# One burst of attention a step, and the squares of q and k as a stage of their own, in a fused attention and gated feed-forward kernel

## The chip, the core and the metric

The kernel runs on one core of a Trainium2 chip. A core has five engines that work from queues of their own: TensorE (PE in the profile; its weight loads are PEld), VectorE (DVE), ScalarE (ACT), GpSimd (POOL) and SyncE (SP), which here issues the transfers. TensorE writes its results to PSUM, from which DVE and ACT read; everything else lies in SBUF, and the inputs, the output and scratch copies in DRAM. The metric is the device time of one execution in microseconds. All times below are of this kind, or are starts and durations from one profiled execution.

## The reference

Two computations follow each other. The first is attention with random features: for 8 batches, 8 heads, 576 positions and 64 numbers a head,

```
q_s, k_s = q * scale, k * scale                # scale = 64 ** -0.25
phi(x)   = exp(x @ omega.T - |x|^2 / 2 - max) / sqrt(128)
kv       = sum over positions of phi(k_s)^T v       # 128 x 64 a head
z        = sum over positions of phi(k_s)           # 128 a head
attn     = (phi(q_s) @ kv) / (phi(q_s) @ z + 1e-6)
```

The maximum is taken over the 128 features of each row. The second is a gated feed-forward network over the 4608 tokens (batch and position) of 512 numbers that attention gives, with 1536 inner columns:

```
g   = x @ w_gate
out = (silu(g) * (x @ w_val)) @ w_out
```

All of it is float32 outside; the kernel does the feed-forward matmuls as three products of a high and a low part each.

## The kernel before

**Steps.** The rows of q and k are cut into groups of 256 rows of a pair of heads (plus a group of rests), and a *step* handles two groups: two of k in the first six steps, then one of q and one of k, at the end two of q. There are 72 steps, and a few more to run out. One group passes through functions that are called in different steps: `load` three steps ahead; `st_transpose` (four transposes on TensorE into the PSUM tile pt, ACT copies it to x, POOL squares the loaded rows into sq); `st_project` (16 small matmuls into pp); `st_max` (DVE sums the squares, L419, takes the maxima of pp, L426, and forms the exponent's bias, L428 and L429); `st_exp` (eight exponentials on ACT, L440). A group of k then goes to `k_accumulate` two steps later (matmuls into kvacc, and where a half of the heads of a batch is complete, `kv_finalize`, in which ACT copies kvacc to kvr, L456). A group of q goes one of two ways. For batches 0 to 3, `q_transpose` (ptq, ACT copies it to qt), a step later `q_mult` (po, with the denominator as a 65th column; DVE forms dn, its reciprocal and the normed rows xn, L590 to L593), and again a step later `q_out` (transposes of xn into xt, from which ACT and DVE make the high and low parts, or ACT a copy xo for DRAM). For batches 4 to 7, `q_den` and `q_norm` do the division with POOL and DVE, from z laid out over all partitions: `kv_finalize` transposes z (zp, L462), ACT copies it, and it goes to DRAM (zd); `load_z` brings it back spread out (zt).

**Two halves.** The first 25 steps (`n < EARLY`) call the functions in the order of the tuple `CLOSE`. From then on the order is `GROUPED`, a *mixed* step: attention's functions, and at each place `SHARE` a share of the feed-forward work, which `give` takes from the generator `stream`, and of the conversion of the weights (`tick`, whose generator `convert_all` gives five DVE operations, L270 to L278, for each piece, between an ACT one, L268, and a POOL one, L280). In a mixed step before the change attention comes in two places: most of it at the head, and `q_norm` and `q_mult` between the third and the fourth SHARE.

**Buffers.** PSUM tiles rotate by tag. `ps_att` has one buffer (tag b: po, zp, and ptq of the first group), `ps_tr` one (tag t: pt, xt), kvacc one (tag kv), pp two (tag pp), the feed-forward tiles three (tag m). A tile is written again only when its readers are done. In SBUF, nat (the loaded rows) has three buffers, sq two, st six.

**Feed-forward.** Tokens come in nine tiles of 512. Five go through `stream`, in visits of 72 matmuls (g and v, L659) and 36 (o, L668, summed by DVE into acc, L697) each. The last four go in two pairs by `pair_rounds`, with seven products instead of eight (L874): DVE adds a kept part to a product (`plus`, L971), and one PSUM tile a takes several products in turn. While the second of the first pair's six visits runs, `next_x` loads the second pair's rows, and after each `one_down` it gives one of eight subtractions (L829) that prepare the seven factors; they are used in that pair's last visit.

**The order of the queues.** The code gives an order of calls. In each engine's queue the instructions stand in an order that the framework makes from that order and from what it takes to be ready; in the trace, an instruction of DVE, ACT or POOL that waits holds those behind it (at 874.75 us DVE has waited 5.30 us for a transfer, with a sum behind it whose product was done).

Of the kernel before, what the change touches and what calls it, by code (L numbers as in the profile page):

```python
# [11 lines left out]
F32 = mybir.dt.float32  # L12
# [4 lines left out]
ALU = mybir.AluOpType  # L17
# [6 lines left out]
def kernel(  # L24
# [73 lines left out]
    def ps_att(name, shape):  # L98
        return ps_a.tile(shape, F32, name=name, tag="b")
# [275 lines left out]
    sts = {}  # L375


    def st_transpose(n):
        if n >= NS:
            return  # L380
        nat = nats.pop(n)
        pt = ps_tr(f"pt_{n}", [P, 2, G])
        for i in range(2):
            for c in range(CH):
                nc.tensor.transpose(  # L385
                    pt[:, i, c * P : (c + 1) * P], nat[:, i, c].rearrange("p h d -> p (h d)"), ident
                )
        x = att.tile([P, 2, G], F32, name=f"x_{n}", tag="x")

        st = att.tile([P, 4, 2, CH, 2], F32, name=f"st_{n}", tag="st", bufs=6)  # L390
        sq = att.tile([P, 2, CH, 2, D], F32, name=f"sq_{n}", tag="sq")
        nc.gpsimd.tensor_tensor(sq, nat, nat, op=ALU.mult)  # L392
        nc.scalar.copy(x, pt)  # L393
        sts[n] = x, st, sq
        return True

    def st_project(n):
        if n >= NS:
            return
        x, st, sq = sts[n]  # L400

        new = ps_moe if n < EARLY and n % 2 else ps_proj
        pp = [new(f"pp{hh}_{n}", [P, 2, CH, M]) for hh in range(2)]
        for i in range(2):
            for c in range(CH):
                for hh in range(2):
                    r = slice(hh * D, (hh + 1) * D)
                    nc.tensor.matmul(  # L408
                        pp[hh][:, i, c, :], x[r, i, c * P : (c + 1) * P], omT[r], start=True, stop=True
                    )  # L410
        sts[n] = st, sq, pp
        return True

    def st_max(n):
        if n >= NS:
            return
        st, sq, pp = sts[n]

        nc.vector.tensor_reduce(  # L419
            st[:, 0].rearrange("p i c h -> p (i c h)"),  # L420
            sq.rearrange("p i c h d -> p (i c h) d"),
            axis=AX.X,
            op=ALU.add,
        )
        for hh in range(2):
            nc.vector.tensor_reduce(st[:, 1, :, :, hh], pp[hh], axis=AX.X, op=ALU.max, negate=True)  # L426
        s0, s1, s2, s3 = (st[:, j].rearrange("p i c h -> p (i c h)") for j in range(4))
        nc.vector.scalar_tensor_tensor(s2, s0, SQC, s1, op0=ALU.mult, op1=ALU.add)  # L428
        nc.vector.scalar_tensor_tensor(s3, s0, -SQC, s2, op0=ALU.mult, op1=ALU.add)  # L429
        return True  # L430

    def st_exp(n):
        if n >= NS:
            return
        st, _, pp = sts.pop(n)
        for i, (kind, b, g) in enumerate(steps[n]):
            ph = att.tile([P, CH, 2 * M], F32, name=f"ph{i}_{n}", tag=f"ph{i}", bufs=3)
            for hh in range(2):
                for c in range(CH):
                    nc.scalar.activation(  # L440
                        ph[:, c, hh * M : (hh + 1) * M], pp[hh][:, i, c, :],
                        AF.Exp, bias=st[:, 3, i, c, hh : hh + 1], scale=1.0,
                    )
            box[kind, b, g] = ph
        return True
# [7 lines left out]
    def kv_finalize(b, a2):  # L453
        acc = kvacc.pop((b, a2))
        raw = att.tile([P, 4, VW], F32, name=f"kvr{b}_{a2}", tag="kvr", bufs=4)
        nc.scalar.copy(raw, acc)  # L456
        for j in range(2):
            kvst[b, 2 * a2 + j] = raw[:, 2 * j : 2 * j + 2, :]
        if b >= BPOOL:

            zp = ps_att(f"zp{b}_{a2}", [4, P])
            nc.tensor.transpose(zp, raw[:, :, D], ident)  # L462
            zs = att.tile([4, P], F32, name=f"zs{b}_{a2}", tag="zs")
            nc.scalar.copy(zs, zp)
            zd = dram.tile([4, P], F32, name=f"zd{b}_{a2}", tag="zd", bufs=4)
            nc.sync.dma_start(zd, zs)
            zds[b, a2] = zd

    zds = {}
    zbc = {}  # L470

    def load_z(n):

        for _, b, g, gr in slots(n, "q"):
            if g == 0 and b >= BPOOL:
                zt = att.tile([P, 2, 4, M], F32, name=f"zt{b}", tag="zt")
                for a2 in range(2):
                    nc.sync.dma_start(
                        zt[:, a2], zds.pop((b, a2)).rearrange("(o h) m -> o h m", o=1).broadcast_to([P, 4, M])
                    )  # L480
                    zbc[b, a2] = zt[:, a2]
# [29 lines left out]
    def q_norm(n):  # L511
        n -= NLAG
        for _, b, g, gr in slots(n, "q"):
            if b < BPOOL:
                continue
            dn = dns.pop((b, g))
            phv = box["q", b, g].rearrange("p c (h m) -> p (c h) m", m=M)
            nc.gpsimd.tensor_tensor(
                phv, phv,
                dn[:, 2].rearrange("p c (h o) -> p (c h) o", o=1).broadcast_to([P, 2 * CH, M]),  # L520
                op=ALU.mult,
            )
# [266 lines left out]
    sevens = {}  # L789

    factors, ahead = {}, {}

    def first_x():

# [26 lines left out]
    def next_x(r):  # L821

        for half, names in ((0, ("b11", "t1")), (1, ("b21", "b22"))):
            for j, name in zip(PAIRS[r], names):
                nc.sync.dma_start(ahead[name], x_dram[j][:, half * CH : (half + 1) * CH, :])
        yield
        for o, a, b in (("t3", "b22", "t1"), ("t1", "t1", "b11"), ("t2", "b22", "t1"), ("t4", "b21", "t2")):
            for c in range(CH):
                nc.vector.tensor_tensor(ahead[o][:, c], ahead[a][:, c], ahead[b][:, c], op=ALU.subtract)  # L829
                yield  # L830

    def new_factors():
# [51 lines left out]
    def pair_rounds(todo):  # L884
# [51 lines left out]
        for vi, (r, k_, pf) in enumerate(pair_visits):  # L936
# [20 lines left out]
            for i, use in ((0, gate), (1, value)):  # L957
# [10 lines left out]

                def plus(n, ps, name):
                    o = sl[n] if i == 0 else kp[:, 3]  # L970
                    nc.vector.tensor_tensor(o, ps, keep[name], op=ALU.add)  # L971
                    use(n, o)

                a, c, d = (ps_w.tile([P, T], F32, name=f"{e}{vi}_{i}", tag="w") for e in "acd")
# [35 lines left out]
    def give(us):  # L1010
# [15 lines left out]
    SHARE = None  # L1026
    CLOSE = (
        st_project,
        q_norm,
        q_out,  # L1030
        lambda n: st_transpose(n + 1),
        q_mult,
        lambda n: k_accumulate(n, 0),
        st_max,
        q_transpose,
        lambda n: k_accumulate(n, 1),
        st_exp,
# [1 line left out]
    )  # L1039
    GROUPED = (  # L1040
        q_out,
        st_project,
        q_transpose,
        lambda n: k_accumulate(n, 0),
        lambda n: k_accumulate(n, 1),
        st_max,
        st_exp,
        q_den,
        lambda n: st_transpose(n + 1),
        SHARE,  # L1050
        SHARE,
        SHARE,
        lambda n: q_norm(n + 1),
        q_mult,
        SHARE,
        SHARE,
        SHARE,
# [6 lines left out]
    for n in range(LAV):  # L1064
        load_v(n)
    load(2)
    st_transpose(0)
    for n in range(NN):
        load(n + LA)
# [56 lines left out]
```

## Time and profile before

| what | value |
|---|---|
| median of 3 runs | 1218.34 us (1216.6 to 1220.92) |
| the profiled execution | 1219.54 us |
| its span, first to last instruction | 1217.8 us |
| mean granted TensorE clock | 0.987 |
| TensorE busy | 1173.9 us, 96% |
| weight loads | 969.5 us, 80% |
| ACT, DVE, POOL busy | 660.9 us (54%), 647.1 us (53%), 585.0 us (48%) |

Rows of the profile name an instruction by its engine, its line (L419), what it writes and reads (st<-sq), and how often it occurs. In a timeline the columns are start, duration, engine, line, operation, and in brackets the engine's idle time before it and what ended that. A table of waits has the waiting line, what it waited for, the total, the number of times and the longest. Matmuls overlap, so that a matmul of 0.39 us may start 0.23 us after the one before, and TensorE's busy share says little by itself; its idle times and the starts of its instructions say more. The granted clock is TensorE's, 1.00 being full speed.

### The profile page before, as it was taken

The page shows a single profiled execution, that of the slowest core. Times are in us where ns is not written, and L with a number is a line of the kernel's source. Part 1 is how long each engine was busy: PE and PEld are TensorE (multiplying, and loading weights), DVE is VectorE, ACT ScalarE, POOL GpSimd, SP SyncE. Part 2 cuts the span into 40 slices and gives each one's busy share as a digit, 9 for nine tenths or more (in the row PEclk, how much of TensorE's full clock was granted, in tenths as well). Part 3 has the DMA queues.
Part 4 walks back from the last instruction along what each step waited for, and adds up shares of the span by engine and source line. Part 5 has one row for each costly group of instructions (what it writes and reads, how often), then busy time and mean ns, then how long its engine had stood idle before and what let it go on. Part 6 is the DMA issues. An engine that isn't in the chain of part 4 may idle for free.

```text
span 1217.8 us, 18846 instructions
## 1 busy us (share of the span) xinstructions
PE 1173.9 (96%) x6705; PEld 969.5 (80%) x6705; DVE 647.1 (53%) x1231; ACT 660.9 (54%) x1461; POOL 585.0 (48%) x500
## 2 busy tenths in 40 slices
PE   6999999999999999999999999999899999999998
PEld 5888887888787678878888877878688888888886
DVE  5588886364656763434333354174545456545544
ACT  4687866574465555466555666353454445454431
POOL 3343442254344645545454585444565553555541
PEclk9799999999999999999999999999999999999999
DMA  6556656253544433244222211334321111312103
GB/s 151 125 132 157 168 146 186 50 153 86 170 113 119 119 86 93 71 112 101 66 62 81 67 60 45 88 103 138 96 55 58 48 49 26 104 52 53 52 18 69
DMA packets 174109, 113.52 MB, mean 93 GB/s; under 512 B 125856, under 2 KB 144320, under 8 KB 174016
## 3 DMA queue, kind: packets, MB, share of 16 engines
q1 hardware_dynamic: 174016, 112.32, 34.1%
q8 instruction: 53, 0.87, 0.3%
q14 instruction: 40, 0.33, 0.1%
HBM read 87.10 MB, written 25.18 MB: 92 GB/s over the span
## 4 chain that ended last, share of the span: by engine, by line
PE 78%; DVE 8%; DMA 5%; POOL 3%; issue 3%; ACT 2%; SPq 1%; POOLq 0%; ACTq 0%; DVEq 0%
PE o L668 21%; PE g L659 11%; PE a L874 10%; PE v L659 10%; PE pp L408 5%; PE c L874 5%; PE kvacc L542 4%; PE ptq L566 3%; PE d L874 2%; PE pt L385 2%; DMA nat<-in_k_dram 2%; PE po L583 2%; PE xt L623 1%; DVE st L426 1%; SPq L343 1%
## 5 line engine op out<-in xcount | busy, mean ns | idle before, releaser
L440 ACT ACTIVATE ph<-pp,st 128x128 f32<-128x128 f32 x576 | 157.5, 390 | 32.8 <-DVE st L429 32.3
L697 DVE TENSOR_TENSOR acc<-o,acc 128x512 f32<-128x512 f32 x140 | 95.8, 685 | 100.5 <-PE o L668 100.3
L392 POOL TENSOR_TENSOR sq<-nat 128x512 f32<-128x512 f32 x72 | 77.2, 1072 | 120.1 <-DMA nat<-in_k_dram 98.7
L426 DVE TENSOR_REDUCE st<-pp 128x4 f32<-128x512 f32 x144 | 93.0, 683 | 68.0 <-PE pp L408 67.9
L251 POOL TENSOR_TENSOR wlo<-wraw,whi 128x512 fp32r<-128x512 f32 x76 | 99.9, 1325 | 55.5 <-ACT whi L250 55.2
L408 PE MATMUL pp<-omT,x 64*128 64x128 f32 x1152 | 97.4, 301 | 5.5 <-ACT x L393 4.5
L668 PE MATMUL o<-whi,hh 128*128 128x512 f32 x240 | 96.6, 402 | 6.3 <-ACT sl L733 3.4
L408 PEld LDWEIGHTS pp<-omT,x 64*128 64x128 f32 x1152 | 79.4, 199 | 24.1 <-issue 11.6
L756 POOL TENSOR_TENSOR hl<-sl,hh 128x512 fp32r<-128x512 f32 x60 | 78.8, 1318 | 37.5 <-ACT hh L755 37.4
L659 PE MATMUL g<-xh,whi 128*128 128x512 f32 x240 | 96.9, 404 | 0.0
L659 PE MATMUL v<-xh,whi 128*128 128x512 f32 x240 | 95.7, 399 | 0.7 <-DVE acc L697 0.7
L668 PE MATMUL o<-whi,hl 128*128 128x512 f32 x240 | 94.4, 393 | 0.9 <-POOL hl L756 0.9
L659 PE MATMUL g<-xl,whi 128*128 128x512 f32 x240 | 94.4, 393 | 0.0
L659 PE MATMUL g<-xh,wlo 128*128 128x512 f32 x240 | 94.4, 393 | 0.0
L668 PE MATMUL o<-wlo,hh 128*128 128x512 f32 x240 | 94.3, 393 | 0.0
L659 PE MATMUL v<-xh,wlo 128*128 128x512 f32 x240 | 93.7, 391 | 0.0
L659 PE MATMUL v<-xl,whi 128*128 128x512 f32 x240 | 93.6, 390 | 0.0
L502 POOL TENSOR_TENSOR jk<-ph,zt 128x512 f32<-128x512 f32 x32 | 41.3, 1295 | 107.0 <-ACT ph L440 106.9
L280 POOL TENSOR_TENSOR wc<-st,wc 128x512 f32<-128x512 f32 x36 | 48.7, 1355 | 90.4 <-DVE wc L278 43.8
L419 DVE TENSOR_REDUCE st<-sq 128x8 f32<-128x512 f32 x72 | 49.0, 681 | 80.6 <-POOL sq L392 80.6
L865 POOL TENSOR_TENSOR wlo<-s,whi 128x512 fp32r<-128x512 f32 x44 | 65.2, 1498 | 33.9 <-DVE late L971 12.1
L865 POOL TENSOR_TENSOR wlo<-wraw,whi 128x256 fp32r<-128x256 f32 (+1 forms) x44 | 45.6, 1036 | 72.9 <-ACT whi L864 72.3
(252 smaller groups left out, 2925.3 us busy)
## 6 DMA issues: line engine op xcount, KB each, us to landing
wraw<-wscr SPq DMA_DIRECT2D x120, 256.0 KB, 2.7
wscr<-wc SPq DMA_DIRECT2D x36, 256.0 KB, 2.4
out_dram<-acc SPq DMA_DIRECT2D x72, 128.0 KB, 2.3
nat<-in_k_dram SPq DMA_DIRECT2D x64, 128.0 KB, 2.9
v<-in_v_dram SPq DMA_DIRECT2D x64, 128.0 KB, 3.3
nat<-in_q_dram SPq DMA_DIRECT2D x64, 128.0 KB, 2.9
st<-in_moe_w_gate_dram SPq DMA_DIRECT2D x12, 512.0 KB, 4.4
st<-in_moe_w_val_dram SPq DMA_DIRECT2D x12, 512.0 KB, 4.9
```

The source lines that it names most:

```text
L251: nc.gpsimd.tensor_tensor(lo, raw, hi.bitcast(F32), op=ALU.subtract)
L392: nc.gpsimd.tensor_tensor(sq, nat, nat, op=ALU.mult)
L408: nc.tensor.matmul(pp[hh][:, i, c, :], x[r, i, c * P : (c + 1) * P], omT[r], start=True, stop=True)
L419: nc.vector.tensor_reduce(st[:, 0].rearrange("p i c h -> p (i c h)"), sq.rearrange("p i c h d -> p (i c h) d"), axis=AX.X, op=ALU.add,)
L426: nc.vector.tensor_reduce(st[:, 1, :, :, hh], pp[hh], axis=AX.X, op=ALU.max, negate=True)
L440: nc.scalar.activation(ph[:, c, hh * M : (hh + 1) * M], pp[hh][:, i, c, :], AF.Exp, bias=st[:, 3, i, c, hh : hh + 1], scale=1.0,)
L659: nc.tensor.matmul(ps, a_[:, ws], b_[:, c, :], start=n == 0, stop=n == 3 * NC - 1)
L668: nc.tensor.matmul(ps, a_[:, ts_], b_, start=first and n == 0, stop=last and n == 2)
L697: nc.vector.tensor_tensor(a_, po, a_, op=ALU.add)
L756: nc.gpsimd.tensor_tensor(hl, h, hh.bitcast(F32), op=ALU.subtract)
L865: nc.gpsimd.tensor_tensor(lo, src_, hi.bitcast(F32), op=ALU.subtract)
L874: nc.tensor.matmul(ps, a_[:, w_], b_[:, c, :], start=start and c == 0 and m == 0, stop=c == CH - 1 and m == 2, skip_group_check=True,)
```

## The change

- `st_square` (POOL's squares, and the tiles st and sq) and `st_sum` (DVE's sums) are taken out of `st_transpose` and `st_max` and become functions of their own, called for step n + 1: in GROUPED the squares behind `st_max` and the sums behind the third SHARE; in CLOSE the squares behind `st_project` and the sums behind `st_max`.
- In GROUPED, `q_mult` moves from between the SHAREs to the place behind `q_out`, and `q_transpose` from ahead of `k_accumulate` to behind it. `q_norm` stays between the SHAREs.
- The transposes of z leave `kv_finalize`: they are noted in `z_todo`, and `z_rows` does them, behind `st_project` in GROUPED, or in `load_z` where z is wanted at once.
- Each subtraction of `next_x` gets a dependency, without a semaphore, on the last sum that `plus` has emitted, so that it stands behind that sum in DVE's queue.

```diff
@@ -375,6 +375,29 @@
     sts = {}
 
 
+    squares = {}
+    def st_square(n):
+        if n >= NS:
+            return
+        st = att.tile([P, 4, 2, CH, 2], F32, name=f"st_{n}", tag="st", bufs=6)
+        sq = att.tile([P, 2, CH, 2, D], F32, name=f"sq_{n}", tag="sq")
+        nc.gpsimd.tensor_tensor(sq, nats[n], nats[n], op=ALU.mult)
+        squares[n] = st, sq
+    def st_sum(n):
+        if n >= NS:
+            return
+        st, sq = squares.get(n)
+        nc.vector.tensor_reduce(
+            st[:, 0].rearrange("p i c h -> p (i c h)"),
+            sq.rearrange("p i c h d -> p (i c h) d"),
+            axis=AX.X,
+            op=ALU.add,
+        )
     def st_transpose(n):
         if n >= NS:
             return
@@ -386,18 +409,14 @@
                     pt[:, i, c * P : (c + 1) * P], nat[:, i, c].rearrange("p h d -> p (h d)"), ident
                 )
         x = att.tile([P, 2, G], F32, name=f"x_{n}", tag="x")
-        st = att.tile([P, 4, 2, CH, 2], F32, name=f"st_{n}", tag="st", bufs=6)
-        sq = att.tile([P, 2, CH, 2, D], F32, name=f"sq_{n}", tag="sq")
-        nc.gpsimd.tensor_tensor(sq, nat, nat, op=ALU.mult)
         nc.scalar.copy(x, pt)
-        sts[n] = x, st, sq
+        sts[n] = x, squares[n][0]
         return True
 
     def st_project(n):
         if n >= NS:
             return
-        x, st, sq = sts[n]
+        x, st = sts[n]
 
         new = ps_moe if n < EARLY and n % 2 else ps_proj
         pp = [new(f"pp{hh}_{n}", [P, 2, CH, M]) for hh in range(2)]
@@ -408,20 +427,14 @@
                     nc.tensor.matmul(
                         pp[hh][:, i, c, :], x[r, i, c * P : (c + 1) * P], omT[r], start=True, stop=True
                     )
-        sts[n] = st, sq, pp
+        sts[n] = st, pp
         return True
 
     def st_max(n):
         if n >= NS:
             return
-        st, sq, pp = sts[n]
-        nc.vector.tensor_reduce(
-            st[:, 0].rearrange("p i c h -> p (i c h)"),
-            sq.rearrange("p i c h d -> p (i c h) d"),
-            axis=AX.X,
-            op=ALU.add,
-        )
+        st, pp = sts[n]
         for hh in range(2):
             nc.vector.tensor_reduce(st[:, 1, :, :, hh], pp[hh], axis=AX.X, op=ALU.max, negate=True)
         s0, s1, s2, s3 = (st[:, j].rearrange("p i c h -> p (i c h)") for j in range(4))
@@ -432,7 +445,7 @@
     def st_exp(n):
         if n >= NS:
             return
-        st, _, pp = sts.pop(n)
+        st, pp = sts.pop(n)
         for i, (kind, b, g) in enumerate(steps[n]):
             ph = att.tile([P, CH, 2 * M], F32, name=f"ph{i}_{n}", tag=f"ph{i}", bufs=3)
             for hh in range(2):
@@ -457,7 +470,12 @@
         for j in range(2):
             kvst[b, 2 * a2 + j] = raw[:, 2 * j : 2 * j + 2, :]
         if b >= BPOOL:
+            z_todo.append((b, a2, raw))
+    def z_rows(_):
+        while z_todo:
+            b, a2, raw = z_todo.pop(0)
             zp = ps_att(f"zp{b}_{a2}", [4, P])
             nc.tensor.transpose(zp, raw[:, :, D], ident)
             zs = att.tile([4, P], F32, name=f"zs{b}_{a2}", tag="zs")
@@ -466,6 +484,7 @@
             nc.sync.dma_start(zd, zs)
             zds[b, a2] = zd
 
+    z_todo = []
     zds = {}
     zbc = {}
 
@@ -473,6 +492,7 @@
 
         for _, b, g, gr in slots(n, "q"):
             if g == 0 and b >= BPOOL:
+                z_rows(n)
                 zt = att.tile([P, 2, 4, M], F32, name=f"zt{b}", tag="zt")
                 for a2 in range(2):
                     nc.sync.dma_start(
@@ -789,6 +809,7 @@
     sevens = {}
 
     factors, ahead = {}, {}
+    latest = [None]
 
     def first_x():
 
@@ -826,7 +847,14 @@
         yield
         for o, a, b in (("t3", "b22", "t1"), ("t1", "t1", "b11"), ("t2", "b22", "t1"), ("t4", "b21", "t2")):
             for c in range(CH):
-                nc.vector.tensor_tensor(ahead[o][:, c], ahead[a][:, c], ahead[b][:, c], op=ALU.subtract)
+                sub = nc.vector.tensor_tensor(ahead[o][:, c], ahead[a][:, c], ahead[b][:, c], op=ALU.subtract)
+                tc.add_manual_dep(
+                    sub.ins,
+                    latest[0].ins.name,
+                    mybir.DependencyInfo(mybir.DependencyClass.NoSync, mybir.DependencyReason.DATA),
+                    reason="TensorE waits for the products' sums, nothing waits for these",
+                )
                 yield
 
     def new_factors():
@@ -968,7 +996,7 @@
 
                 def plus(n, ps, name):
                     o = sl[n] if i == 0 else kp[:, 3]
-                    nc.vector.tensor_tensor(o, ps, keep[name], op=ALU.add)
+                    latest[0] = nc.vector.tensor_tensor(o, ps, keep[name], op=ALU.add)
                     use(n, o)
 
                 a, c, d = (ps_w.tile([P, T], F32, name=f"{e}{vi}_{i}", tag="w") for e in "acd")
@@ -1026,12 +1054,14 @@
     SHARE = None
     CLOSE = (
         st_project,
+        lambda n: st_square(n + 1),
         q_norm,
         q_out,
         lambda n: st_transpose(n + 1),
         q_mult,
         lambda n: k_accumulate(n, 0),
         st_max,
+        lambda n: st_sum(n + 1),
         q_transpose,
         lambda n: k_accumulate(n, 1),
         st_exp,
@@ -1039,19 +1069,22 @@
     )
     GROUPED = (
         q_out,
+        q_mult,
         st_project,
-        q_transpose,
+        z_rows,
         lambda n: k_accumulate(n, 0),
         lambda n: k_accumulate(n, 1),
+        q_transpose,
         st_max,
+        lambda n: st_square(n + 1),
         st_exp,
         q_den,
         lambda n: st_transpose(n + 1),
         SHARE,
         SHARE,
         SHARE,
+        lambda n: st_sum(n + 1),
         lambda n: q_norm(n + 1),
-        q_mult,
         SHARE,
         SHARE,
         SHARE,
@@ -1064,6 +1097,8 @@
     for n in range(LAV):
         load_v(n)
     load(2)
+    st_square(0)
+    st_sum(0)
     st_transpose(0)
     for n in range(NN):
         load(n + LA)
```

## The prediction

> **What bounds the kernel now.** I read the stages first, then TensorE's own waits, then the queues of the engines for which it waits. The page's first line:
>
> ```profile
> span 1217.8 us, 18846 instructions
> ```
>
> Busy time by stage: after the stretch come PE, PEld, DVE, ACT, POOL in us, then the granted clock.
>
> ```profile
> 60.00:150.00 90.00, 85.69 (x759) 75.22 (x759) 78.93 (x198) 72.04 (x213) 38.08 (x33) 1.00 0.58 150
> 205.00:350.00 145.00, 141.39 (x893) 118.37 (x889) 75.52 (x156) 86.29 (x198) 54.94 (x45) 0.99 0.42 120
> 350.00:440.00 90.00, 84.78 (x511) 68.32 (x507) 63.25 (x113) 45.04 (x100) 47.38 (x38) 0.98 0.42 122
> 440.00:750.00 310.00, 306.05 (x1849) 247.37 (x1848) 124.55 (x255) 182.99 (x406) 164.09 (x145) 0.99 0.29 75
> 820.00:1217.80 397.80, 388.56 (x1703) 319.91 (x1702) 198.26 (x310) 172.49 (x303) 202.83 (x160) 0.99 0.23 63
> ```
>
> Up to 150 us, attention alone (CLOSE), DVE is busy 78.93 of 90 us: reordering there can win little. From 205 us TensorE is the bound, and what can be won is its idle time: 3.6 us to 350, 5.2 to 440, 4.0 to 750, 9.2 from 820. The changed q_mult (steps 25 to 43) lies between 139 and 371 us, the changed subtractions near 880. TensorE's waits from 150 to 440 us, then three from later (total, times, longest), then single rows with the idle time in brackets:
>
> ```profile
> PE xt L616 <- DVE xn L593: 4.0, 5, 1.1
> PE pt L385 <- DVE xl L645: 0.7, 1, 0.7
> PE zp L462 <- ACT kvr L456: 1.3, 1, 1.3
> PEld zp L462 <- ACT kvr L456: 3.4, 8, 1.5
> PE a L874 <- DVE sl2k L971: 3.2, 1, 3.2
> ...
> 388.78 0.50 PE L668 MATMUL o<-whi,hh 128*128 128x512 f32 x1 [2.32 <-DVE acc L697]
> 420.92 0.50 PE L668 MATMUL o<-whi,hh 128*128 128x512 f32 x1 [2.82 <-ACT sl L733]
> 454.57 0.66 PE L385 MATMUL pt<-ident,nat 128*128 128x128 f32 x4 [2.49 <-ACT xo L638]
> ```
>
> The first five are touched by the change, the last three are not, at least by name.
>
> **The change, part by part.** *Subtractions of next_x (L829).* DVE's queue around the longest wait, two of the eight subtractions left out, and the window after it:
>
> ```profile
> 874.75 1.24 DVE L850 TENSOR_TENSOR s<-wraw 128x256 f32<-128x256 f32 x1 [5.30 <-DMA wraw<-wscr]
> 877.03 1.28 DVE L829 TENSOR_TENSOR late<-late,late 128x512 f32<-128x512 f32 x2
> ...
> 879.44 0.69 DVE L971 TENSOR_TENSOR sl0k<-c,late 128x512 f32<-128x512 f32 x1
> 880.04 2.49 DVE L829 TENSOR_TENSOR late<-late,late 128x512 f32<-128x512 f32 x4
> 882.45 0.69 DVE L971 TENSOR_TENSOR sl2k<-a,late 128x512 f32<-128x512 f32 x1
> ...
> 882.70:886.10 3.40, 2.91 (x7) 2.36 (x8) 1.03 (x2) 2.15 (x5) 3.40 (x3) 0.50 0.24 77
> ```
>
> DVE waits 5.30 us for a weight transfer; behind it run all eight subtractions in a bunch (x2, x2 and x4, the four of 2.49 us making 0.6 each, some 5 us), and two sums that TensorE needs wait among them. With the dependency each subtraction follows the sum last emitted at its place, so the eight spread over some eight products. The two sums then follow the weights' last operation at 877.1 and, with one subtraction between, end near 879.2, before TensorE's stop at about 880. The 3.2 us go, and with them the window at clock 0.50: 3.4 us at half rate cost 1.7. Term: **-4.9** (0 if the bunch still lands ahead). The subtractions stay 5 us of DVE in a stage where it is half idle; nothing waits for them until the last visit of the pair. By the rows, a half-rate window followed the waits of 3.2 and 2.49 us, but not that of 2.32 (next rows).
>
> ```profile
> 389.00:392.40 3.40, 3.40 (x25) 2.35 (x26) 1.28 (x3) 0.37 (x1) 1.04 (x1) 1.00 0.00 0
> 456.00:459.40 3.40, 3.40 (x10) 2.63 (x9) 0.00 (x0) 3.38 (x9) 0.88 (x1) 0.50 0.74 190
> ```
>
> The Trainium skill, "TensorE: Matmul & The Clock Gate", section "What's actually happening", has the clock halved after an idle window of about 3.4 us. By that figure the 3.2 us wait costs no window, this term is 3.2, and the sum below is 1.7 higher. Here the trace differs, with halving after 2.49 us, and decides.
>
> *Rows of z (z_rows).* Eight small transposes leave k_accumulate and run a step later, when the copy kvr is long made. What they waited is at most 3.4 us (the PEld row), at least the one 1.3 us stall; but in that step the accumulation behind it needs the same one-buffer PSUM tile and the same copy, so part stays. The transposition that now follows k_accumulate fills some of it. Term: **-1.3** (0 to -3.4). The issue of zd on SP and a 0.25 us copy on ACT move with it. For b = 7 the flush comes only in load_z, about a step later than before, and POOL's multiplication by zt waits; I take nothing for it, at most 3 us.
>
> *q_mult into the burst.* Its po matmuls and ptq share a one-buffer PSUM tile (tag b). Now po stood between MoE matmuls, and its reader xn was due at the next burst. One late step, from its po to its maxima; then the same two rows, projection and maxima, of the first and the last of the twelve late steps:
>
> ```profile
> 301.18 1.00 PE L583 MATMUL po<-kvr,qt 128*128 128x65 f32 x8
> 308.48 0.41 PE L616 MATMUL xt<-ident,xn 128*128 128x128 f32 x2 [0.77 <-DVE xn L593]
> 308.82 1.16 PE L408 MATMUL pp<-omT,x 64*128 64x128 f32 x16
> 309.92 0.66 PE L566 MATMUL ptq<-ident,ph 128*128 128x128 f32 x4
> 310.41 1.00 PE L542 MATMUL kvacc<-v,ph 128*128 128x65 f32 x8
> 311.25 0.61 PE L385 MATMUL pt<-ident,nat 128*128 128x128 f32 x4
> 313.75 1.28 DVE L426 TENSOR_REDUCE st<-pp 128x4 f32<-128x512 f32 x2
> ...
> 152.52 1.16 PE L408 MATMUL pp<-omT,x 64*128 64x128 f32 x16
> 154.07 0.68 DVE L426 TENSOR_REDUCE st<-pp 128x4 f32<-128x512 f32 x1
> 348.98 1.16 PE L408 MATMUL pp<-omT,x 64*128 64x128 f32 x16
> 351.30 1.28 DVE L426 TENSOR_REDUCE st<-pp 128x4 f32<-128x512 f32 x2
> ```
>
> What goes: xn is made a step ahead of xt, so the five waits, 4.0 us, vanish; pt gets 0.8 us more for xl, 0.7 us. Term **-4.7**. Entering and leaving MoE once less is worth under 0.1 us a step by the starts, 1.00 us of po against 0.81 between its neighbours; I count nothing.
>
> What comes: ptq waits until DVE has read po. Cover is the projection (309.92 - 308.82 = 1.10) and the accumulation (311.25 - 310.41 = 0.84), 1.94 us; the readers dn, reciprocal and xn take about 0.75. DVE in time: no wait. DVE as late as it is for the maxima now: at 308.82 they begin 3.83 us after the projection, and that, less 0.1, would be the wait (1.10 + 3.83 + 0.75 - 1.94 = 3.74). Over the eighteen steps that have both q_mult and ptq, twelve are late (the first by 0.45 us, the last by 1.22), and the waits add up to 17.5. The queue ahead is weight conversion that ACT or a transfer delayed, and it blocks whatever stands behind it. So 0 to +17.5. The readers are ready 1.1 us before the maxima and so stand ahead of some of the backlog, and each wait lets DVE catch up; on the other side, the present xn waits cost 4.0 in all under a longer cover (5.5 us in the row above: po's end at 302.2 to 307.7), and the new cover is less. I take a value little above that row: **+5.5**.
>
> *Squares and sums.* The stage is new in the code; what counts is where they ran.
>
> ```profile
> L419 DVE TENSOR_REDUCE st<-sq x72: 655/686/690, 5.8 to 705.6; 128x8 f32<-128x512 f32 x72
> L408 PE MATMUL pp<-omT,x x1152: 272/272/580, 7.0 to 745.9; 64*128 64x128 f32 x192
> 386.37 1.04 POOL L392 TENSOR_TENSOR sq<-nat 128x512 f32<-128x512 f32 x1 [2.28 <-DMA nat<-in_k_dram]
> 387.44 0.69 DVE L419 TENSOR_REDUCE st<-sq 128x8 f32<-128x512 f32 x1 [2.63 <-POOL sq L392]
> 388.05 0.68 DVE L697 TENSOR_TENSOR acc<-o,acc 128x512 f32<-128x512 f32 x1
> ```
>
> The last sum starts at 705.6, 40 us ahead of the last projection: the order in the queues is made by what is ready, and squares and sums already run three steps ahead of need, right behind the load. The same 72 squares and 72 sums remain. The load of nat holds POOL, the square holds DVE, and acc, for which TensorE waits 2.32 us at 388.78, stands behind the sum. A stage one step ahead doesn't forbid this. Term **0**: -2.3 if that wait goes, +1.0 if a square comes ahead of something urgent on POOL.
>
> *CLOSE* gets two more places; its ticks are spread over 13 instead of 11, and DVE's work is the same: 0.
>
> **Sum:** -4.9 - 1.3 - 4.7 + 5.5 = -5.4. The profiled execution took 1219.54 us (span 1217.8 and 1.7 around it), so 1214.1 on its scale; it stands 1.2 above the median of the runs, 1218.34, where the sum gives 1212.9. I say **1213**. About 0.3%, 3.7 us, can be told from no change.
>
> **The rivals.** *A, slower:* ptq waits for xn in tag b. At the full 17.5 us the sum is +6.6; two or three of the waits (3.7, 2.3, 2.3, 2.2) would be long enough for a half-rate window, 1.7 each, so 1225 to 1229. It decides from about 11 us on (then nothing is won), and makes the kernel slower by over 0.3% from 14.6. For it: the twelve late steps. Against: the readers' earlier place. The Trainium skill, same page, section "A second HAM failure mode: psum-queue depth-cycling", speaks for it: short waits on a PSUM buffer between groups of matmuls keep the clock falling back. The trace has such falls only after the waits named above; no run here shows what many short waits do.
>
> *B, more is won:* the new wait stays near 0 and the waits at 388.78, 420.92 and 454.57 (2.32 + 2.82 + 2.49, and a half-rate window behind each of the longer two, 3.4) don't recur in the new layout: -5.4 - 5.5 = -10.9 with the first alone, 1207; with half of these 11.0 us, 1202. For it: those waits come from chance meetings of late transfers. Against: the load, the conversion and the table switches that make them remain, and can meet elsewhere.
>
> *C, the change doesn't do what it says:* the order follows readiness, the subtractions still come in a bunch, and the burst wins what it loses: -1.3 - 4.7 + 5.5, so 1218, the same.
>
> **Chances.** The forecast (1209 to 1217) 0.43, B 0.25, C 0.15, A 0.17. Two thirds of the forecast's span lies below 1214.7, so faster: 0.28 + 0.25 + 0.01 = 0.54. Same: 0.15 of the forecast, 0.13 of C, 0.01 of A, 0.29. Slower: 0.17. The range drops the ends of A and B: 1203 to 1224.
>
> **What would show it.** Right: no L829 bunch before L971, no wait or 0.50 window near 880; no row "xt <- DVE xn" past 150 us; zp a step later without a wait; a new row "ptq <- DVE xn" of some 5 us in total, in steps 25 to 42; sums still 40 us ahead of the projections, and POOL still waiting for nat. Wrong: ptq's wait over 11 us (A), none at all and fewer waits between 380 and 460 (B), or CLOSE, up to 150 us, longer or shorter by over 3 us, for which I have no term.

## The result: slower by 1.6%, and the profile after

| | median | range | times |
|---|---|---|---|
| before | 1217.8 us | 1216.6 to 1220.92 | 4 |
| after | 1237.94 us | 1232.7 to 1241.01 | 4 |

(The median of before is now that of four times, not of three.) The ratio is 1.0157, with a 95% interval of 1.0114 to 1.0200. The profiled execution of after took 1232.7 us, the lowest of its four times. Its span, and the stages that the change was not to touch or was to shorten:

```profile
span 1230.6 us, 18850 instructions
```

```profile
440.00:750.00 310.00, 306.36 (x1862) 248.21 (x1862) 127.04 (x260) 178.39 (x401) 166.46 (x146) 1.00 0.32 82
835.00:1230.60 395.60, 387.50 (x1705) 319.14 (x1703) 204.36 (x310) 172.36 (x303) 205.18 (x160) 1.00 0.23 63
```

Both run at clock 1.00 with 3.6 and 8.1 us in which TensorE is idle, against 4.0 and 9.2 before: nothing is lost there. The loss is in the stretch in which attention and the feed-forward work are mixed. The next windows go from the first projection of step 36 to that of step 40, and from step 44 to step 47, so that they hold the same work in both kernels. Before:

```profile
263.20:322.00 58.80, 56.63 (x346) 47.12 (x345) 33.67 (x65) 33.59 (x73) 21.52 (x18) 1.00 0.43 125
376.60:425.30 48.70, 43.48 (x247) 34.03 (x246) 32.30 (x53) 25.68 (x56) 27.83 (x22) 0.96 0.40 116
```

After:

```profile
262.10:330.30 68.20, 61.79 (x346) 52.92 (x345) 35.18 (x67) 33.94 (x75) 21.27 (x17) 0.90 0.39 113
384.20:443.60 59.40, 46.39 (x249) 36.79 (x248) 34.46 (x55) 26.56 (x56) 28.84 (x23) 0.86 0.32 90
```

The same matmuls take 9.4 and 10.7 us more, at a clock of 0.90 for 1.00 and of 0.86 for 0.96. Steps 25 to 32 add another 6.2 (by the starts of their projections, 139.5 to 214.8 us before, 132.3 to 213.8 after). That is 26.3; the rest from step 25 on is 6.3 us shorter, 2.5 of it in the pair stage (838.6 to 1217.8 before, 853.9 to 1230.6 after). In all, step 25 to the end took 1078.3 us before and 1098.3 after. This difference of 20.0 fits the medians, 20.1 apart. (The two spans are only 12.8 apart, because in these two executions step 25 began 7.2 us earlier in after; the last section returns to that.)

What TensorE waits for between 150 and 440 us, in after:

```profile
PE ptq L586 <- DVE xn L613: 12.6, 8, 3.3
PE o L688 <- DVE acc L717: 6.9, 1, 6.9
PE ptq L586 <- ACT zs L482: 6.1, 1, 6.1
```

Its longest single waits there (in brackets), and then the windows that follow them:

```profile
171.03 0.91 PE L586 MATMUL ptq<-ident,ph 128*128 128x128 f32 x4 [2.68 <-DVE xn L613]
267.02 1.09 PE L586 MATMUL ptq<-ident,ph 128*128 128x128 f32 x4 [2.75 <-DVE xn L613]
301.74 1.09 PE L586 MATMUL ptq<-ident,ph 128*128 128x128 f32 x4 [3.31 <-DVE xn L613]
401.03 0.79 PE L688 MATMUL o<-whi,hh 128*128 128x512 f32 x1 [6.91 <-DVE acc L717]
429.72 1.09 PE L586 MATMUL ptq<-ident,ph 128*128 128x128 f32 x4 [6.08 <-ACT zs L482]
```

```profile
171.20:174.60 3.40, 3.40 (x13) 3.02 (x13) 3.37 (x9) 2.30 (x7) 1.01 (x1) 0.51 0.04 10
266.80:273.60 6.80, 6.58 (x24) 5.93 (x25) 1.60 (x5) 4.53 (x11) 0.75 (x1) 0.50 0.62 182
301.00:307.80 6.80, 6.06 (x19) 5.13 (x20) 4.26 (x8) 3.46 (x11) 4.67 (x4) 0.50 0.31 82
396.50:406.70 10.20, 5.67 (x17) 3.59 (x19) 2.71 (x6) 0.36 (x1) 2.08 (x2) 0.50 0.12 28
427.20:434.00 6.80, 4.28 (x14) 3.75 (x15) 4.77 (x7) 3.29 (x11) 3.91 (x4) 0.50 0.58 182
```

Each of the five waits comes with a stretch at half clock, 34.0 us together. Half of that, 17.0, is the most it can have cost: the long ones begin while TensorE is still idle (396.50 against the end of the wait at 401.03).

**Why ptq waits for xn.** DVE's queue in step 36 of after, and under it what POOL does meanwhile. po is finished, and its three readers stand behind one piece of weight conversion:

```profile
260.29 1.56 DVE L270 TENSOR_SCALAR wc<-wc 128x512 f32<-128x512 f32 x1
261.89 1.38 DVE L272 TENSOR_SCALAR wc<-wc 128x512 int32<-128x512 int32 x1
263.30 1.64 DVE L274 SCALAR_TENSOR_TENSOR st<-st,wc 128x512 int32<-128x512 int32 x1
...
266.05 0.15 DVE L610 TENSOR_SCALAR dn<-po 128x4 f32<-128x4 f32 x1
...
266.45 0.42 DVE L613 TENSOR_TENSOR xn<-po,dn 128x256 f32<-128x256 f32 x1
...
260.27 2.71 POOL L251 TENSOR_TENSOR wlo<-wraw,whi 128x512 fp32r<-128x512 f32 x2
262.94 1.45 POOL L776 TENSOR_TENSOR hl<-sl,hh 128x512 fp32r<-128x512 f32 x1
```

The readers themselves take 0.8 us. ptq starts at 267.02, once xn (begun at 266.45) is written and the one buffer of tag b is free.

The conversion itself is slow here. In the trace of after, the 115 of its 180 operations on DVE during which POOL runs nothing take at most 0.70 us each; all 26 that take more than 1 us overlap an operation of POOL, by at least 0.46 us. (Another 30 overlap one and stay under 0.70 us.) The three rows above take 4.58 us, against some 1.5 us for the same three at the median where POOL rests; the difference of 3 us is more than the wait of 2.75. That POOL's work is the cause fits all these rows, but no run takes it away, so it is not shown.

**Why ptq waits for zs.** ACT and DVE before the stop at 429.72. zp stands in the same buffer, and its copy zs is the last thing in a line:

```profile
426.77 1.40 DVE L276 TENSOR_SCALAR wc<-st 128x512 int32<-128x512 int32 x1
428.08 0.68 DVE L772 TENSOR_TENSOR sl<-v,sl 128x512 f32<-128x512 f32 x1
...
428.80 0.62 ACT L775 CAST hh<-sl 128x512 fp32r<-128x512 f32 x1 [4.08 <-DVE sl L772]
429.32 0.25 ACT L482 COPY zs<-zp 4x128 f32<-4x128 f32 x1
```

A copy of 0.25 us is held by a cast that doesn't concern it, the cast by a product on DVE, the product by conversion, here too with operations of 1.40 us and more.

**Why o waits for acc.** The load of nat, the square that needs it, the sum, and acc, on SP, POOL and DVE:

```profile
395.26 0.64 SPq L343 DMA_DIRECT2D nat<-in_k_dram  x1
398.55 1.04 POOL L387 TENSOR_TENSOR sq<-nat 128x512 f32<-128x512 f32 x1 [5.44 <-DMA nat<-in_k_dram]
399.62 0.69 DVE L394 TENSOR_REDUCE st<-sq 128x8 f32<-128x512 f32 x1 [5.79 <-POOL sq L387]
400.29 0.69 DVE L717 TENSOR_TENSOR acc<-o,acc 128x512 f32<-128x512 f32 x1
```

This is the chain that the prediction showed for before at 386 to 389 us, with 6.9 us in place of 2.3. In before the load was issued earlier in its step (step 44 began at 376.6, the load is 6.1 us later; in after 384.2 and 11.1):

```profile
382.68 0.64 SPq L343 DMA_DIRECT2D nat<-in_k_dram  x1
```

### The profile page after: what moved, and what is told of

The parts are those of the page before. It is cut to its first block, busy times and chain, and to the rows that moved or that the text cites. A ratio compares the mean times of both kernels' runs of the same rounds, so it can differ in the third digit from the quotient of the medians.

```text
span 1230.6 us, 18850 instructions
## 1 busy us (share of the span) xinstructions
PE 1172.3 (95%) x6705; PEld 972.2 (79%) x6705; DVE 647.6 (53%) x1231; ACT 658.5 (54%) x1461; POOL 587.4 (48%) x500
## 4 chain that ended last, share of the span: by engine, by line
PE 74%; DVE 8%; DMA 5%; POOL 5%; issue 3%; ACT 2%; SPq 2%; POOLq 0%; ACTq 0%; DVEq 0%
PE o L688 22%; PE g L679 10%; PE a L902 10%; PE v L679 10%; PE c L902 5%; PE pp L427 4%; PE kvacc L562 4%; DMA nat<-in_k_dram 3%; PE d L902 3%; PE ptq L586 2%; PE pt L408 2%; DMA st<-in_moe_w_gate_dram 2%; PE xt L643 1%; POOL sq L387 1%; SPq L343 1%
## 5 line engine op out<-in xcount | busy, mean ns | idle before, releaser
L394 DVE TENSOR_REDUCE st<-sq 128x8 f32<-128x512 f32 x72 | 49.1, 681 | 100.7 <-POOL sq L387 100.7
```

## The experiments

Three explanations were open. One: q_mult beside q_transpose makes po and ptq meet in the one buffer of tag b. Two: it is no matter of the buffer; a burst of more work crowds ACT and DVE, and whatever TensorE needs from them comes late. Three: one of the other parts (the stage of squares and sums, the rows of z, the dependency) does it. Each experiment is timed beside before on the same chip; a ratio is to before, with its 95% interval. After was not timed again with them, so its 1.0157 comes from another comparison with before. Lines are those of after where nothing else is said; in the kernels with the hold they are shifted by ten or eleven, and in the one with the dependency alone they are near those of before.

### One part of the change alone

**The dependency alone**, added to before:

```diff
-                nc.vector.tensor_tensor(ahead[o][:, c], ahead[a][:, c], ahead[b][:, c], op=ALU.subtract)
+                sub = nc.vector.tensor_tensor(ahead[o][:, c], ahead[a][:, c], ahead[b][:, c], op=ALU.subtract)
+                tc.add_manual_dep(
+                    sub.ins, latest[0].ins.name,
...
-                    nc.vector.tensor_tensor(o, ps, keep[name], op=ALU.add)
+                    latest[0] = nc.vector.tensor_tensor(o, ps, keep[name], op=ALU.add)
```

> The kernel before with the dependency of the eight subtractions alone. If the 3.2 us wait and its half-rate window are simply won: 4.9 us faster than before, 1213. In the changed kernel the stage of the pairs (first L874 matmul to the last) was only 2.5 us shorter, with a wait of 1.95 for ACT's copy in place: then 1215 to 1216. All orders up to 800 us are those of before, so nothing else may change.

Measured: 1218.46 us, ratio 0.9994 (0.9958 to 1.0029). The wait of 3.2 us for sl2k is gone, but a new one follows three products later, for a copy on ACT:

```profile
905.29 0.50 PE L881 MATMUL a<-t2hi,whi 128*128 128x512 f32 x1 [1.94 <-ACT late L974]
```

The pair stage (840.0 to 1216.8) is 2.4 us shorter than in before, as in after (2.5). By the timing alone this can't be told from nothing, and neither expected time (1213, or 1215 to 1216) was reached.

**The stage of squares and sums alone**, in the layout of before (z inside `kv_finalize`, no dependency):

```diff
     GROUPED = (
...
         st_max,
+        lambda n: st_square(n + 1),
         st_exp,
...
         SHARE,
+        lambda n: st_sum(n + 1),
         lambda n: q_norm(n + 1),
         q_mult,
```

> The kernel before with squares and sums as a stage of their own alone (z transposed in kv_finalize, q_mult between the SHAREs, no dependency). Theory T and my prediction: the queues' order hardly changes, 1215 to 1221, and POOL still waits some 100 us for nat and DVE some 80 us for the squares. Rival L: 1225 or above, with waits for acc of more than 5 us near 390 us.

Measured: 1218.62 us, ratio 1.0000 (0.9968 to 1.0032). Of POOL's 500 instructions in the trace 2 stand in another place in its queue than before, of DVE's 1231 some 42. The place in the code moved; the place in the queue did not.

**All but the move of q_mult and q_transpose:**

```diff
         q_out,
-        q_mult,
         st_project,
         z_rows,
+        q_transpose,
         lambda n: k_accumulate(n, 0),
         lambda n: k_accumulate(n, 1),
-        q_transpose,
...
         lambda n: q_norm(n + 1),
+        q_mult,
         SHARE,
```

> The changed kernel with q_mult back between the SHAREs and q_transpose back ahead of k_accumulate; squares, z_rows and the dependency stay as changed. Theory T (PSUM tag b: in one burst ptq waits until DVE has read po, 12.6 us in 8 waits, and the half-rate windows behind those waits): the waits ptq <- DVE xn vanish, half-rate time after 130 us falls from 34 us to about 10, and the time returns to 1211 to 1219. Rival L (the stage of squares and sums puts the wait for the load of nat into DVE's queue, 6.9 us before acc at 401 us and a 10.2 us half-rate window): time stays at 1228 or above and the wait of acc stays.

Measured: 1219.93 us, ratio 1.0013 (0.9990 to 1.0036). So the third explanation falls: the loss comes with the move of q_mult and q_transpose, 1.0013 to 1.0157, or 1.44% (17.5 us). ptq no longer waits for xn. It still waits 4.5 us for zs, in two places, so that wait comes with z_rows and not with the burst.

### What it is about the burst

**The same burst, ptq ahead of po:**

```diff
         q_out,
-        q_mult,
         st_project,
-        z_rows,
+        q_transpose,
         lambda n: k_accumulate(n, 0),
         lambda n: k_accumulate(n, 1),
-        q_transpose,
+        z_rows,
+        q_mult,
         st_max,
```

> The changed kernel, still one burst, but ptq ahead of po: q_out, st_project, q_transpose, k_accumulate twice, z_rows, q_mult. po then waits for ACT's copy of ptq only, and DVE has the rest of the step to read po. Theory T: what costs is the order inside tag b, not the one burst; no wait for xn at ptq, at most a few us of po <- ACT qt, 1210 to 1220. If the one burst itself costs (one long stretch without MoE matmuls in which DVE and ACT fall behind): 1228 or above. Rival L: 1228 or above, with acc's wait.

Measured: 1234.58 us, ratio 1.0121 (1.0088 to 1.0153). TensorE's waits, 150 to 440 us:

```profile
PE po L603 <- ACT qt L588: 6.4, 5, 3.3
PE o L688 <- DVE acc L717: 5.7, 1, 5.7
```

With the order turned round, po waits for the reader of ptq: half the total. The wait for acc stays. The expected 1210 to 1220 did not come: the order inside tag b is at most a part of what costs. Steps 25 to 40 take 193.6 us (136.6 to 330.2), against 182.5 in before and 198.0 in after.

**q_transpose between the SHAREs**, where q_mult was, so that po and ptq are apart again:

```diff
         lambda n: k_accumulate(n, 1),
-        q_transpose,
         st_max,
...
         lambda n: q_norm(n + 1),
+        q_transpose,
         SHARE,
```

> The changed kernel with q_transpose between the SHAREs (where q_mult was before), q_mult in the burst, so that po and ptq of tag b stand a few MoE matmul groups apart on both sides. Theory T2 (two tiles of the one-buffer tag b in one burst, whichever comes first, make TensorE wait for a reader on a busy engine: DVE xn in the changed kernel, ACT qt with the order turned): no wait at ptq for xn and none at po for qt over 2 us in all, 1214 to 1222. Rival B (po's work in the burst crowds DVE and ACT there, whatever tag it uses): 1228 or above.

Measured: 1231.03 us, ratio 1.0107 (1.0069 to 1.0144). The wait of ptq for xn is gone, and two others have grown:

```profile
PE o L688 <- DVE acc L717: 9.4, 2, 6.4
PE pt L408 <- ACT xo L658: 5.5, 3, 4.5
```

The expected 1214 to 1222 did not come. The waits that have grown are for readers on ACT and DVE of tiles in other buffers. But this run moves ptq as well, and does not show that po in the burst alone makes these readers late; the runs with po in another buffer, below, keep the burst whole and speak against it for steps 25 to 40.

**The rows of z back inside `kv_finalize`**, with the burst of after, and then with q_transpose between the SHAREs as in the last experiment:

```diff
             z_todo.append((b, a2, raw))
+            z_rows(0)
...
         st_project,
-        z_rows,
```

> The changed kernel with z transposed inside kv_finalize again; the one burst, squares and dependency stay. In the changed kernel ptq waited 6.1 us for ACT's copy of z out of PSUM tag b, with 6.8 us at half rate behind it. If that is a cost of z_rows: those 6 to 9 us come back, 1226 to 1231. If z_rows is harmless and the wait only moves: 1234 to 1240. In both cases ptq <- DVE xn keeps 8 to 16 us.

Measured: 1246.34 us, ratio 1.0200 (1.0150 to 1.0249). Now ptq waits for xn 9.6 us, acc costs 7.2, and zp itself waits for xn 2.3, since it needs the buffer of po.

> As the kernel with q_transpose between the SHAREs, and z transposed inside kv_finalize again. If both costs lie in tag b: nothing waits for zs, 1211 to 1219, the fastest so far. If z_rows does not matter there: the same as that kernel within 3 us.

Measured: 1236.73 us, ratio 1.0129 (1.0067 to 1.0191), beside 1.0107 without that edit. Both times lie outside what was expected. In both pairs the intervals overlap: z_rows does not cause the loss, and what it gains is not settled by these runs.

**po in another PSUM buffer**, one of the three that the feed-forward tiles use (tag m), the order as in after:

```diff
-            po = ps_att(f"po{b}_{g}", [P, CH, 2, VW])
+            po = (ps_att if n + MLAG < EARLY else ps_moe)(f"po{b}_{g}", [P, CH, 2, VW])
```

> The changed kernel, one burst in its order, but po lies in one of the three PSUM buffers of the feed-forward work (tag m), so ptq needs not wait for xn. Theory T2: ptq <- DVE xn gone (12.6 us and its half-rate windows), but the feed-forward tiles have a buffer less while po waits to be read, which may bring waits for silu or acc: 1222 to 1234. If po's buffer is not what costs: 1235 or above with the same late spots (steps 25 to 32 and 36 to 40).

Measured: 1223.87 us, ratio 1.0031 (1.0003 to 1.0058). Waits of TensorE, and then the two windows of step 36 to 40 and 44 to 47:

```profile
PE ptq L586 <- ACT zs L482: 7.8, 2, 6.0
PE o L688 <- DVE acc L717: 6.9, 1, 6.9
```

```profile
259.20:315.80 56.60, 56.00 (x346) 47.67 (x345) 32.08 (x63) 33.62 (x75) 20.38 (x16) 1.00 0.40 115
372.60:430.60 58.00, 45.08 (x249) 36.16 (x248) 34.96 (x56) 26.61 (x56) 28.93 (x23) 0.88 0.33 91
```

This parts the two losses. Steps 36 to 40 fall from 68.2 to 56.6 us, below before's 58.8, at full clock; steps 25 to 40 in all from 198.0 (132.3 to 330.3) to 181.3 (134.5 to 315.8), 16.7 us. That is the price of po in tag b in these two executions, waits and half clock together; the two ratios, 1.0157 and 1.0031, put it at about 15. Steps 44 to 47 stay at 58.0 (59.4 in after, 48.7 in before): there acc and zs are late as in after.

**zp there as well:**

```diff
-            zp = ps_att(f"zp{b}_{a2}", [4, P])
+            zp = ps_moe(f"zp{b}_{a2}", [4, P])
```

> The changed kernel with po and zp both in the feed-forward work's PSUM tag m, so that nothing in the burst waits in tag b. Theory T2: the waits for zs (7.8 us with po alone in tag m, and half-rate windows) go too, and only acc's 6.9 us and its windows stay: 1214 to 1222. If the waits move to the feed-forward tiles: 1223 or above.

Measured: 1222.41 us, ratio 0.9995 (0.9955 to 1.0034). The wait for zs is gone, but steps 44 to 47 hardly gain: acc still costs its 6.9 us, and a later o (at 424.09) waits 2.73 us for sl, which ACT makes. The row of steps 44 to 47:

```profile
371.20:428.50 57.30, 46.28 (x249) 35.79 (x248) 33.72 (x53) 26.29 (x56) 28.83 (x23) 0.88 0.31 87
```

With both tiles out of the shared buffer, the change as a whole costs nothing that can be measured, and wins nothing. Steps 44 to 47 are still 8.6 us longer than in before; gains elsewhere make up for it.

### The stage made to come one step ahead

What was left was acc, held by a sum that ran three steps ahead of its need. So the square and the sum of each step n were held behind the last DVE operation (the bias) of step n - 1, by the same kind of dependency that the change gives the subtractions:

```diff
+    def behind(n, op):
+        if n > EARLY:
+            tc.add_manual_dep(
+                op.ins, biases[n - 1].ins.name,
...
-        nc.gpsimd.tensor_tensor(sq, nats[n], nats[n], op=ALU.mult)
+        behind(n, nc.gpsimd.tensor_tensor(sq, nats[n], nats[n], op=ALU.mult))
```

and the same for the sum. First with q_mult in its old place and z inside `kv_finalize`:

> The kernel before (two places of attention, z inside kv_finalize) with the dependency of the subtractions, squares as a stage, and each square and sum from step 26 on held behind the bias of the step before by a dependency without a semaphore, so that they really run one step ahead, not three. Theory L (a sum that waits for a square that waits for a load of nat holds DVE's queue, and TensorE then waits for acc, xn or ptq): DVE's and POOL's waits for squares and nat fall to some 10 us after 150 us, TensorE's waits for acc and xn shrink, 1206 to 1214, faster than before. If those waits of DVE and POOL cover nothing that TensorE needs: 1215 to 1221, the same.

Measured: 1205.48 us, ratio 0.9872 (0.9814 to 0.9930). The waits for acc add up to 0.5 us between 150 and 440 us, against 2.9 in before.

Then after with the hold alone, po and zp still in tag b:

> The changed kernel with squares and sums held one step ahead, po and zp in tag b as changed. Together with the three others this separates tag b from the load of nat. If both add: the waits at ptq stay (some 12 us for xn, 6 for zs), acc's goes, 1222 to 1232. If DVE is late for xn because of the sums, too: ptq's waits shrink and it comes to 1218 or below.

Measured: 1210.23 us, ratio 0.9907 (0.9875 to 0.9938), 2.5% below after. Two of the three waits are still there, each a little shorter; the mean clock from 150 to 440 us is 0.99:

```profile
PE ptq L596 <- DVE xn L623: 9.1, 8, 2.1
PE ptq L596 <- ACT zs L492: 5.0, 1, 5.0
```

```profile
150.00:440.00 290.00, 273.54 (x1732) 231.36 (x1733) 181.22 (x357) 169.20 (x381) 123.34 (x99) 0.99 0.44 127
```

In after the clock in the same row is 0.94. Here the eight waits of at most 2.1 us for xn leave the clock alone; in after, the three longest of the eight did not.

The expected 1222 to 1232, for the case that the two costs add, did not come. The burst costs 1.44% without the hold (1.0013 against 1.0157). With it, the burst (0.9907) and the old places (0.9872, with z inside `kv_finalize`) have intervals that overlap. So it seems that the cost of the burst hangs on how late DVE is, and not on tag b alone.

Last, the hold with po and zp in tag m:

> As the kernel with po and zp in tag m, and squares and sums held one step ahead. If the 6.9 us before acc come from the sum that waits for the load of nat: they go, with some 5 us of half-rate loss, 1204 to 1213, faster than both kernels. If something else holds DVE there: within 3 us of the kernel without the hold.

Measured: 1200.86 us, ratio 0.9834 (0.9779 to 0.9889), the fastest of all. What the hold does is seen in the waits of POOL and DVE over the whole span. In after:

```profile
POOL sq L387 <- DMA nat<-in_k_dram: 106.0, 36, 14.8
...
DVE st L394 <- POOL sq L387: 100.7, 40, 8.5
```

(In before they were 98.7 and 80.6.) In this kernel:

```profile
POOL sq L397 <- DMA nat<-in_k_dram: 43.5, 15, 5.3
DVE st L404 <- POOL sq L397: 19.5, 10, 5.8
```

DVE no longer stands 100.7 us behind squares that wait for a transfer, and what is queued behind it gets through. The load itself is not earlier: in this kernel it is issued at 376.76, 9.9 us into step 44 (which begins at 366.9), not much less than the 11.1 of after.

Not tried: the hold with q_mult in its old place and po in tag m, and the hold without the dependency of the subtractions.

## Why the prediction was wrong, point by point

**The step that failed** is "What comes: ptq waits until DVE has read po", with its "+5.5" out of 0 to 17.5. The mechanism was the right one and its size was not. The wait measured 12.6 us in eight places, past the 11 us from which rival A decides, and the 5.5 had no half-rate window in it. The price of po in tag b, from the run that changes only that, is 16.7 us in steps 25 to 40. Of the 20.0 us that after loses from step 25 on, steps 25 to 40 make 15.5 (198.0 against 182.5), steps 44 to 47 10.7, and the rest wins 6.2. I had argued that the three readers, ready 1.1 us before the maxima, stand ahead of part of the backlog. In step 36 they do stand ahead of the maxima, but the piece of conversion was already in front of both, and 3 us longer than its operations take elsewhere.

**Rival A** named the right mechanism and was too low as well, at 1225 to 1229. It allowed two or three windows of 3.4 us. The three longest ptq waits for xn were followed by 3.4, 6.8 and 6.8. The prediction's remark that the clock of before falls only after the waits it names is a misreading: the same trace has a stretch of 17.1 us at 39.60 and one of 3.4 at 203.40, both shown in the last section, and the second followed two waits of about 1 us.

**z_rows, "-1.3".** The stall of zp for kvr went, but the moved zp left its buffer to a copy on ACT that came 6.1 us late, with 6.8 us at half clock around its end. I had looked only at the copy that zp waits for, not at the one that must read it before ptq. The sign of the whole term isn't settled: z back inside `kv_finalize` was not clearly slower in either pair.

**The neighbours** are the second step that failed. Under "Squares and sums" I took the wait for acc at 388.78 as 2.32 us that would stay, or go. It grew to 6.9 us, with 10.2 us at half clock around it, and its longest was 5.7 to 7.2 in every kernel with q_mult in the burst and no hold; in those with q_mult in its old place and no hold it was at most 2.9. With the hold it is 0.4 or 0.5, or not in the list at all. In the profile the load of nat is issued later in its step there. Why it is, I can only argue: SP issues it behind a store and fetches of weights whose conversion slipped. No run separates that.

**xn ahead of xt, "-4.7".** Right as to the row: "xt <- DVE xn" no longer stands among the waits between 150 and 440 us. In after no gain is left of it, since ptq needed the same reader sooner. With po in tag m, where ptq does not need it, steps 25 to 40 are 1.2 us shorter than in before (181.3 against 182.5).

**The subtractions, "-4.9".** Right as to the mechanism. DVE's queue in after, with one subtraction (L850) between the two sums (L999):

```profile
892.48 0.68 DVE L999 TENSOR_TENSOR sl0k<-c,late 128x512 f32<-128x512 f32 x1
893.08 0.68 DVE L850 TENSOR_TENSOR late<-late,late 128x512 f32<-128x512 f32 x1
893.68 0.68 DVE L999 TENSOR_TENSOR sl2k<-a,late 128x512 f32<-128x512 f32 x1
```

No wait for sl2k is left and no window at half clock. The size is half: a wait of 1.9 us for ACT's copy follows (1.94 in the row of the dependency alone), and the stage gained 2.4 to 2.5 us.

**Squares and sums, 0,** and rival C's premise, that the order follows readiness: right, ratio 1.0000 for that part alone. I took from it that nothing was to be won there. With the order forced, the same stage is worth 1.6% (0.9995 to 0.9834): the three steps of lead were not harmless. With them DVE stood 80 to 100 us behind squares, and without them some 20.

**CLOSE, 0:** the early half of the variants, all with the same or nearly the same order there, ends anywhere between 132.3 and 142.0 us; the two executions with before's own order end it at 139.5 and 141.8. The prediction called over 3 us of difference here a sign of being wrong, and after is 7.2 us shorter, but no effect of CLOSE can be told from that spread.

## What to carry to other kernels

Before a PSUM write is moved next to another in a one-buffer tag, follow every reader of that buffer to its place in its engine's queue, and price the wait with what it does to the clock; a buffer from another tag took away 16.7 us here for one changed line, while with the hold in place that line and the one for zp together made 0.7% (0.9907 to 0.9834), by intervals that overlap. Where a framework orders the queues by readiness, a function's place in the code is only a wish: an operation that depends on a transfer can run steps early and hold a whole in-order queue, and a dependency without a semaphore on a recent instruction of the engine that suffers puts it where it was meant to be. Test the parts of a change one by one: here one part cost 1.4%, and another that was worth nothing as written gave 1.6% once its order was enforced.

## What was not expected of the hardware

The stretches at half clock come in multiples of 3.4 us: 3.4, 6.8 and 10.2 in after, and one of 17.1 early in before, here with the mean clock in the eighth column:

```profile
39.60:56.70 17.10, 17.10 (x98) 15.85 (x94) 7.38 (x16) 8.79 (x28) 2.71 (x3) 0.50 0.39 102
```

TensorE is busy in all of it, so up to 8.5 us were lost. In after, a wait of 2.68 us was followed by 3.4 at half clock, those of 2.75 and 3.31 by 6.8, and the one of 6.91 by 10.2; waits up to 2.1 us in the kernel with the hold alone left the mean at 0.99. But the length of a single wait does not settle it. In before, two waits of about 1 us, some 1.5 us apart, were followed by 3.4 us at half clock:

```profile
201.77 0.48 PE L408 MATMUL pp<-omT,x 64*128 64x128 f32 x2 [1.05 <-ACT ph L440]
203.32 0.56 PE L616 MATMUL xt<-ident,xn 128*128 128x128 f32 x2 [1.06 <-DVE xn L593]
...
203.40:206.80 3.40, 3.40 (x21) 2.86 (x22) 1.50 (x4) 0.53 (x2) 1.86 (x2) 0.51 0.97 292
```

The Trainium skill, "TensorE: Matmul & The Clock Gate", section "A second HAM failure mode: psum-queue depth-cycling", tells of a kernel that goes through PSUM buffers in turn, and in which TensorE idles briefly between groups of matmuls often enough that the clock falls back again and again. The trace of after agrees in part: 12.6 us of such waits went with 17.0 us of half clock, all of it at the three longest of the eight.

In the early half, such stretches lie elsewhere in each execution. From 30 us to the start of step 25, the dependency alone had a mean clock of 0.92 over 111.8 us, 8.9 us lost; the stage alone 0.98 over 102.3 us, 2.0 lost. These 6.9 us are most of the 9.5 between their starts of step 25, 141.8 and 132.3.
